# Batch 0 in three blocks of two query tiles, and the hash constant as an exp bias

## The chip, the cores and the metric

The kernel runs on one core of a Trainium2 chip. The time is device microseconds (us) of one execution. TensorE is PE in the profile (PEld its weight loads), VectorE DVE, ScalarE ACT, GpSimd POOL, SyncE SP; SPq is SP's issuing of transfers.

## The reference

Four batches of attention with 8 heads, 768 tokens and 64 dimensions. A query sees only the keys whose six hash bits equal its own. The result is the input of a gated feed-forward layer.

```python
q_bits = (einsum('bhsd,dk->bhsk', q, proj) > 0);  k_bits = likewise
mask   = q_bucket[:, :, :, None] == k_bucket[:, :, None, :]
attn   = softmax(where(mask, q @ k.T / 8, -1e9))
x      = (attn @ v) as [3072 tokens, 512]
out    = x + sigmoid(x @ w_res) * ((gelu(x @ w_gate) * (x @ w_val)) @ w_out)   # d_ff = 1536
```

## The kernel before

Each head has an augmented operand: 64 rows of q or k, 6 rows of hash bits as +-0.5, and a seventh row with a constant. One matmul gives the scaled score plus a bonus for equal bits, and an exp with a large scale makes every unequal pair vanish. Two heads (a pair) are prepared together: 4 pairs in a batch, 16 in all.

The kernel doesn't run its operations as written. `op` records each with a cost and the keys that it reads and writes; at the end a small list scheduler in the kernel plans them with these costs and gives out one order for each engine. On the chip each engine goes through its order and waits on semaphores. So a change of a cost, a key or a latency can change the order of everything.

```python
RINGS = dict(sc=2, av=1, mm=3, qs=3, ks=3, vs=3, trT=4, e=8, bits=4, ...)
LAT = 0.22
...
# the sign column that also makes the constant hash row; the tiles are 4 or 8 bytes wide
for nm, lay in (("shift0", ...), ("shift1", ...)):
    ind = const.tile([P, 2], FP32, name="ind" + nm)
    ...
    sh = const.tile([P, 1], FP32, name=nm)
...
def load_blocks(n):                       # q and k of batches 1 to 3: pieces of 32 floats
    for nm, src in (("q", q), ("k", k)):
        s = stage_of(nm, n, [P, S // Q, Q])
        for hh in range(2):
            for c in range(D // Q):
                load(nm, "SP", g, s, ..., src[b, 2*j+hh, :, c*Q:(c+1)*Q].rearrange("(m p) d -> p m d", p=Q), 0.65, 0.6)
...
def prep_blocks(n):                       # DVE transposes, PE hashes, DVE makes bits, SP moves them
    for side, nm in enumerate("qk"):
        op("DVE", 0.9, nc.vector.transpose(trT()[:, side, :], s()...))
    ...
    for i in range(4):
        op("SP", 0.75, nc.sync.dma_start(a[D:KAUG, :, i*CH:(i+1)*CH], bits()[32*i:32*i+NR]),
           r=[(bits, 0), (bits, 1)],
           w=[("aug", n % NAUG, hh, i // 2, i % 2, "b") for hh in range(2)], size=0.15)
...
# scores of two key tiles against half of the queries (384), then exp
op("ACT", 0.715, nc.scalar.activation(e(), sp()[:, :, 0:CH], AF.Exp, scale=EXPS), r=[sp], w=[e], table="exp")
...
# every batch has two blocks of three query tiles; beside the attention of one block PE does
# the feed-forward of the block before it, which starts with the gates
def end_block(u):
    transpose_x(u)
    for m in range(KF):
        gate(u, m)
    ff = feed_forward(u)
```

The softmax here doesn't subtract the row's maximum and nothing guards it: scores larger than these inputs give would overflow.

## Time and profile before

| | before |
|---|---|
| time | 358.78 us median of 3 (358.62 to 359.25) |
| profiled span | 358.0 us |
| PE, ACT, DVE busy | 343.7, 239.3, 194.4 us |
| first gate matmul | 39.31 us |
| starts of the gates of the next blocks | 82.58, 127.81, 168.58, 211.15, 251.92, 290.87, 328.14 us |

The starts of the gates cut the span into stages of one block each, 40.77 us in the later batches where PE does not wait (the last three are shorter); reading PE's busy time and the length of each stage tells where PE worked and where it idled. Two more views matter for what follows: the stages between the first gates and the gates of batch 1, and the queue of transfers that SP issues. In the stage lines the columns are the stretch, its length, then busy time (and instructions) of PE, weight load, DVE, ACT and POOL, the granted clock, the DMA share and GB/s.

```profile
39.31:82.58 43.27, 42.98 (x415) 25.26 (x413) 29.82 (x48) 30.50 (x45) 3.32 (x4) 1.00 1.04 155
82.58:127.81 45.23, 42.32 (x403) 24.45 (x399) 30.90 (x49) 31.81 (x45) 4.46 (x4) 1.00 1.04 153
```

The queue lines give packets, megabytes, and the time that the packets took as a share of 16 engines' span:

```profile
q1 hardware_dynamic: 101762, 25.54, 38.3%
```

PE idles 3.20 of these 88.50 us, and 2.42 of that is the one stall on xT. The DMA share is 1.04 in both stages.

### The profile page before, as it was taken

Reading aid. Unit: us, or ns where it says so; the run is one execution under the profiler, and the core shown is the slowest. Engines: PE = TensorE matmul, PEld = TensorE weight load, DVE = VectorE, ACT = ScalarE, POOL = GpSimd, SP = SyncE. Lnnn points to the kernel's source line nnn. Section 1 sums busy time; section 2 is a strip of 40 time slices with the busy share of each in tenths; the row PEclk is TensorE's granted clock in tenths of the full one; section 3 lists DMA queues with packets and bytes.
Section 4 is the critical chain, followed back from the end, with each engine's and each line's share of the span. In section 5 each row is a group of like instructions: output and inputs, shape, how many; then the busy total and the mean of one; then the engine's idle time right before and its main releaser. Section 6 shows DMA issues by size and latency. Waiting matters only on the chain.

```text
span 358.0 us, 7849 instructions
## 1 busy us (share of the span) xinstructions
PE 343.7 (96%) x3183; PEld 205.7 (57%) x3183; DVE 194.4 (54%) x356; ACT 239.3 (67%) x344; POOL 24.2 (7%) x35
## 2 busy tenths in 40 slices
PE   7879999999999979999899999999999999999995
PEld 3546665556565546655465566655666566655653
DVE  5897137997794565858063453734153333524353
ACT  2579887558767568676676678685887778776410
POOL 0543001100100100011000000000000000000000
PEclk9999999999999999999999999999999999999999
DMA  7969999779999969920000010000000010001002
GB/s 239 333 124 198 202 169 157 122 126 167 197 117 120 182 111 190 149 64 34 31 1 7 31 66 0 3 33 32 35 0 3 32 59 2 0 31 51 10 2 88
DMA packets 105381, 31.47 MB, mean 88 GB/s; under 512 B 95274, under 2 KB 101378, under 8 KB 105346
## 3 DMA queue, kind: packets, MB, share of 16 engines
q1 hardware_dynamic: 101762, 25.54, 38.3%
q0 software_dynamic: 3280, 5.24, 8.3%
q8 instruction: 25, 0.41, 0.5%
q10 hardware_dynamic: 304, 0.20, 0.2%
q14 instruction: 10, 0.08, 0.1%
HBM read 29.36 MB, written 6.29 MB: 100 GB/s over the span
## 4 chain that ended last, share of the span: by engine, by line
PE 83%; DVE 5%; DMA 4%; ACT 4%; SPq 2%; issue 1%; DVEq 0%; ACTq 0%
PE mm L604 17%; PE mm L619 17%; PE mm L644 16%; PE sc L534 15%; PE av L558 8%; PE mm L631 5%; DMA ks<-in_k_dram 3%; ACT e L538 3%; PE mm L495 2%; SPq L247 2%; PE mm L587 1%; DMA qs<-in_q_dram 1%; DVE aug L397 1%; DVE aug L419 1%; DVE bits L409 1%
## 5 line engine op out<-in xcount | busy, mean ns | idle before, releaser
L538 ACT ACTIVATE e<-sc 128x768 bf16<-128x768 f32 x192 | 150.0, 810 | 57.7 <-PE sc L534 57.6
L534 PE MATMUL sc<-aug 71*128 71x384 bf16 x384 | 91.6, 326 | 1.0 <-ACT e L538 0.7
L622 DVE TENSOR_TENSOR gh<-mm,gh 128x384 bf16<-128x384 f32 x96 | 53.0, 555 | 71.2 <-PE mm L619 58.8
L619 PE MATMUL mm<-xT,wv 128*128 128x384 bf16 x384 | 72.0, 326 | 0.0
L644 PE MATMUL mm<-wo,gh 128*128 128x512 bf16 (+1 forms) x300 | 71.9, 371 | 0.0
L558 PEld LDWEIGHTS <-e 128*128 128x128 bf16 x1152 | 56.2, 97 | 24.6 <-issue 3.0
L604 PE MATMUL mm<-xT,wg 128*128 128x384 bf16 x384 | 65.4, 326 | 3.9 <-DVE xT L593 2.4
L558 PE MATMUL av<-vaug,e 128*128 128x65 bf16 x1152 | 61.7, 193 | 2.1 <-DVE xtok L572 2.1
L607 ACT ACTIVATE gh<-mm 128x384 bf16<-128x384 f32 x96 | 45.7, 491 | 15.8 <-PE mm L604 15.5
L534 PEld LDWEIGHTS <-aug 71*128 71x128 bf16 x384 | 34.8, 98 | 31.5 <-issue 6.8
L604 PEld LDWEIGHTS <-wg 128*128 128x128 bf16 x384 | 36.7, 98 | 27.7 <-DVE xT L593 2.5
L619 PEld LDWEIGHTS <-wv 128*128 128x128 bf16 x384 | 34.7, 98 | 23.5 <-issue 3.7
L644 PEld LDWEIGHTS <-gh 128*128 128x128 bf16 x300 | 26.6, 98 | 22.1
L652 DVE SCALAR_TENSOR_TENSOR y<-th,mm 128x512 f32<-128x512 bf16 (+1 forms) x25 | 16.6, 662 | 38.3 <-PE mm L644 29.5
L634 ACT ACTIVATE th<-mm 128x512 bf16<-128x512 f32 x24 | 14.3, 597 | 17.5 <-PE mm L631 17.5
L631 PE MATMUL mm<-wr,xT 128*128 128x512 bf16 x96 | 24.7, 379 | 0.0
L361 POOL CAST vaug<-vs 128x768 bf16<-128x768 f32 x16 | 15.0, 935 | 138.9 <-DMA vs<-in_v_dram 81.5
L510 DVE TENSOR_SCALAR aug<-trT 64x1536 bf16<-64x1536 f32 x24 | 22.8, 951 | 2.4 <-PE sc L534 2.0
L502 DVE TENSOR_SCALAR bits<-mm,shift 128x384 bf16<-128x384 f32 x24 | 13.7, 613 | 13.7 <-PE mm L495 13.4
L572 DVE TENSOR_TENSOR xtok<-av,rec 128x384 bf16<-128x384 f32 x32 | 17.8, 557 | 1.1
L487 DVE STREAM_TRANSPOSE trT<-ks 128x768 f32<-128x768 f32 x12 | 11.5, 957 | 11.8 <-DMA ks<-in_k_dram 11.8
L654 DVE SCALAR_TENSOR_TENSOR o<-y,xtok 128x512 f32<-128x512 f32 (+1 forms) x25 | 16.8, 670 | 0.8
(52 smaller groups left out, 159.0 us busy)
## 6 DMA issues: line engine op xcount, KB each, us to landing
vs<-in_v_dram SPq DMA_DIRECT2D x16, 384.0 KB
out_dram<-o SPq DMA_DIRECT2D x23, 256.0 KB
qs<-in_q_dram SPq DMA_DIRECT2D x48, 96.0 KB
ks<-in_k_dram SPq DMA_DIRECT2D x48, 96.0 KB
wg<-in_moe_w_gate_dram POOLq DMA_DIRECT2D x4, 384.0 KB, 7.9
wv<-in_moe_w_val_dram POOLq DMA_DIRECT2D x4, 384.0 KB, 8.7
wo<-in_moe_w_out_dram POOLq DMA_DIRECT2D x4, 384.0 KB, 16.4
qs<-in_q_dram SPq DMA_DIRECT2D x3, 384.0 KB
```

Of the source, the lines that this page charges most:

```text
L510: lambda hh=hh: nc.vector.tensor_scalar_mul(a[0:D, hh, :], trT()[hh * D:(hh + 1) * D].rearrange("d s n -> d (s n)"), QKS),
L534: nc.tensor.matmul(sp()[:, x, 0:CH], a[:, S + jt * P:S + (jt + 1) * P], a[:, c * CH:(c + 1) * CH], start=True, stop=True)
L538: op("ACT", 0.715, lambda: nc.scalar.activation(e(), sp()[:, :, 0:CH], AF.Exp, scale=EXPS), r=[sp], w=[e], table="exp")
L558: nc.tensor.matmul(av()[:, o:o + D + 1], e()[:, x, t * P:(t + 1) * P], va[:, 2 * j + hh, TS[b][jt], :], start=(first and x == 0 and t == 0 ...
L572: op("DVE", 0.48, lambda: nc.vector.tensor_mul(xt()[:, :, j * P:(j + 1) * P].rearrange("p t (h d) -> p h t d", h=2), view()[:, :, :, 0:D], ...
L604: nc.tensor.matmul(ps()[:, 0:CH], wg[:, kk, m * P:(m + 1) * P], x()[:, kk, :], start=(kk == 0), stop=(kk == KM - 1))
L607: op("ACT", 0.385, lambda: nc.scalar.activation(g()[:, m, :], ps()[:, 0:CH], AF.Gelu), r=[ps], w=[(g, m)], table="gelu")
L619: nc.tensor.matmul(ps()[:, 0:CH], wv[:, kk, m * P:(m + 1) * P], x()[:, kk, :], start=(kk == 0), stop=(kk == KM - 1))
L622: op("DVE", 0.46, lambda m=m, ps=ps: nc.vector.tensor_mul(g()[:, m, :], ps()[:, 0:CH], g()[:, m, :]), r=[ps], w=[(g, m)])
L631: nc.tensor.matmul(rps(), x()[:, kk, t * P:(t + 1) * P], wr[:, kk, :], start=(kk == 0), stop=(kk == KM - 1))
L644: nc.tensor.matmul(ps()[:, 0:W], g()[:, kk, t * P:(t + 1) * P], wo[:, kk, cols], start=(kk == 0), stop=(kk == KF - 1))
L654: op("DVE", 0.6 / parts, lambda y=y, o=o, t=t, cols=cols, W=W: nc.vector.scalar_tensor_tensor(o()[:, 0:W], y()[:, 0:W], 0.5, xt()[:, t, co ...
```

## The change

The intent is to let the feed-forward start earlier. Batch 0 is cut into three blocks of two query tiles, so that the first block's attention ends sooner; only the queries of the first block must be ready for it, the others are prepared later; the constant hash row gives way to a bias in exp. In the plan, short transfers land 3.5 us after their issue, and the latency between engines goes from 0.22 to 0.26.

```diff
-    NR = NBITS + 1
-    KAUG = D + NR
+    blocks = [(0, c, 2) for c in range(T // 2)] + [(b, c, TC) for b in range(1, B) for c in range(2)]
+    KAUG = D + NBITS
-    RINGS = dict(sc=2, av=1, mm=3, qs=3, ks=3, vs=3, ...
+    RINGS = dict(sc=2, av=1, mm=3, qs=4, ks=3, vs=3, ...
-    LAT = 0.22
+    LAT = 0.26
...
-                    wire = max(wire, o.end + 0.9) + o.size
-                    o.land = wire + 0.9
+                    if o.size > 0.2:
+                        wire = max(wire, o.end + 0.9) + o.size
+                        o.land = wire + 0.9
+                    else:
+                        o.land = o.end + 3.5
...
-    shifts = [] ...                       # the eight instructions and four small tiles of the sign column
+    ebias = const.tile([P, 1], FP32, name="ebias")
+    nc.vector.memset(ebias, -EXPS * NBITS / 4)
...
+    OLD = ["p0", "p1", "late", "h0", "h1", "late0", "late1"]
...                                        # prep_tokens: keys and first queries, then the late queries
-               w=[("aug", n % NAUG, hh, i // 2, i % 2, "b") for hh in range(2)], size=0.15)
+               w=keys_of(n, range(2), OLD + [("q%d", "k%d")[i // 2] % (i % 2)], "b"), size=0.15)
...
-        ... AF.Exp, scale=EXPS)
+        ... AF.Exp, bias=ebias, scale=EXPS)
...
-        loads.setdefault(max(LB, begin[n] - 14), []).append(n)
+        loads.setdefault(max(LB, begin[n] - (24 if n < 2 * NPAIR else 14)), []).append(n)
```

## The prediction

> **What bounds the kernel now.** I read the page's busy line and slices first, then a table of stretches, then the timeline of the first 45 us, then the list of PE waits after 35 us.
>
> ```profile
> PE 343.7 (96%) x3183; PEld 205.7 (57%) x3183; DVE 194.4 (54%) x356; ACT 239.3 (67%) x344; POOL 24.2 (7%) x35
> DMA  7969999779999969920000010000000010001002
> 12.00:20.00 8.00, 7.16 (x107) 4.89 (x107) 7.61 (x17) 4.67 (x8) 2.69 (x4) 1.00 1.09 293
> 20.00:30.00 10.00, 7.83 (x110) 5.34 (x108) 9.59 (x23) 7.16 (x11) 6.39 (x10) 1.00 0.70 126
> ...
> 40.00:80.00 40.00, 39.71 (x377) 23.01 (x376) 27.19 (x45) 28.58 (x42) 3.24 (x4) 1.00 1.05 152
> 120.00:160.00 40.00, 37.58 (x339) 22.52 (x337) 25.86 (x42) 27.74 (x40) 4.03 (x4) 1.00 0.87 141
> 200.00:240.00 40.00, 40.00 (x378) 23.89 (x377) 19.04 (x34) 28.65 (x42) 0.00 (x0) 1.00 0.07 23
> ```
>
> The columns of the stretches are length, then busy time of PE, weight load, DVE, ACT and POOL, the clock, the DMA share, GB/s. Two regimes show. From 40 us PE has no gap worth the name (40.00 of 40 from 200 to 240): PE is the bound, DVE and ACT have room. Before 40 us PE is not the bound although it looks busy, because 72 + 11 of its matmuls there are keep-warm ones that compute nothing; DVE is (9.59 of 10).
>
> ```profile
> 27.37 10.46 ACT L538 ACTIVATE e<-sc 128x768 bf16<-128x768 f32 x14 [2.39 <-PE sc L534]
> 28.11 1.49 DVE L419 COPY aug<-bits 7x384 bf16<-7x384 bf16 x4
> 39.31 0.81 PE L604 MATMUL mm<-xT,wg 128*128 128x384 bf16 x4
> PE mm L604 <- DVE xT L593: 2.4, 1, 2.4
> PE mm L604 <- ACT gh L607: 1.5, 1, 1.5
> L538 ACT ACTIVATE e<-sc 128x768 bf16<-128x768 f32 x192 | 150.0, 810 | 57.7 <-PE sc L534 57.6
> ```
>
> So the prologue has two legs: DVE prepares the four head pairs until 29.6 us, then ACT works off 14 exps back to back (10.46/14 = 0.747 us each) until 37.8, and the first gate matmul, the first feed-forward work that can fill PE, starts at 39.31. After that PE idles 2.4 us once at 125 us (DVE stood behind a late k transfer), 1.5 us once at 170 us, under 1 us elsewhere, and 3.7 us in the tail. Time = start of the gates + PE work left + these stalls.
>
> **What the Trainium skill says.** (1) "TensorE: Matmul & The Clock Gate", "Wait — 56ns, not 53.3ns?": a warm matmul takes N/2.4 ns plus about 2.5 ns. The chain shows 36 gate matmuls of 384 columns in 5.85 us, 162.5 ns each = 160 + 2.5: agrees, so 256 columns should take 109.2 ns. (2) "ScalarE: Activation LUTs", "What ACT_TABLE_LOAD costs": a table load takes about 1283 ns; the trace has 1283 ns (x8 and x7). (3) The same section: 0.833 ns per element plus 186 ns with an immediate bias, and each [128,1] pointer operand adds about 93 ns. The trace has 810 ns at 768 columns and 491 at 384: slope 0.831, fixed part 172, so the exps now run with an immediate bias. The change hands exp a [128,1] tile. No run here shows that cost yet. (4) "VectorE: DVE Perf Modes", "Mode 2×_2P": single-source work from SBUF can go two elements a cycle, from PSUM not. The trace agrees: casts from SBUF gain 0.62 ns per column (599 ns at 768, 360 at 384), evictions from PSUM 1.05 (685 at 512, 550 at 384).
>
> **The change part by part.**
>
> *Removed at the start:* eight small DVE instructions for the sign column, about 1 us between 1.3 and 2.3 us. DVE then waits for the first transpose until 4.86 anyway: worth 0. One hash row less (71 to 70 partitions) changes no instruction's length: 0.
>
> *Preparation on DVE.* For one pair the first part is now two casts of 64x1024, two bit tests of 256 and four moves of 512. From the rates above: 2 x 0.76 + 2 x 0.48 + 4 x 0.36 = 3.9 us; before it was 4 casts, 2 bit tests of 0.61 and 4 moves, about 4.8. Pair 0 (evictions, six half-size casts and so on) I sum to 6.1. To the end of the last pair's first part: 6.1 + 3 x 3.9 + 0.6 for one normalisation = 18.4 us. The same sum for the kernel before gives 23.1 and took 24.7 (4.9 to 29.6), so I expect about 20 and an end near 25. But the built order shows that DVE then prepares the late queries of pairs 0, 1 and 2 before it can evict the second x transpose: 3 x (2 casts 0.88 + 2 bit tests 0.66) + two evictions 1.4 + four normalisations 2.4 + two xT copies 0.8 = 9.2. So DVE is at about 34 when xT is complete; in the kernel before it was there at 40.1 (39.51 + 0.56). **Gates about 6 us earlier, at 33.3.** ACT doesn't forbid it: 24 exps of 512 columns at 0.535 us (0.747 less 256 x 0.83 ns), or 0.63 with the pointer bias, are 13 to 15 us in place of 18.
>
> *PE work that moves behind the gates.* The built order has, ahead of the first gate, 52 scores of 384 and 144 av matmuls before, 56 of 256 and 96 after. Scores: 52 x 162.5 = 8.45 us against 56 x 109.2 = 6.1; totals are 62.4 and 62.5, so 2.4 us more is left. Av (0.18 us per six in the timeline, 30 ns each): 48 more = 1.4. Four x transposes 0.2. Pair 3's late transposes and hash 0.75. The extra fixed 2.5 ns on 48 gate and 48 value matmuls 0.25. **Sum +5.1 us of PE work after the gates.** Net of these two terms: about -1 us. That is the centre of my argument: a shorter first block is no gain in itself, because its attention would have been useful filler that now has to be done later.
>
> *ACT in the region of batch 0.* Three small blocks in place of two: 24 more exps, one more pair of table loads (2.6 us), 12 more gelus, and 93 ns on all 216 exps (20 us if the page holds). In a small block PE has: gates 5.2 + values 5.2 + residual 1.7 + output 5.2 + scores 5.2 + av 2.9 + transposes 0.4 = 26 us and some preparation; ACT has 24 x 0.69 + 12 x 0.38 + 2 x 0.6 + 2.6 + 0.5 = 25.4. So ACT goes from 28.6 of 40 to nearly level with PE for three blocks. PE issues in order and the score ring has two buffers, so I expect 2 to 3 us of new PE waits there, plus up to 1 us at the additional boundary (the built order puts 18 keep-warm matmuls behind the first 12 gates). In the full blocks ACT rises by 24 x 0.093 = 2.2 to about 31 of 40: hidden.
>
> *Transfers.* DMA is full (share about 1.05) from 35 to 140 us in both. Loads of batch 1 are issued 24 steps ahead in place of 14 and get two small blocks, some 54 us in place of 42. The stall at 125 us should shrink or go: -2. Against it, DVE now has batch 1's first transpose right after the first block's 12 products; if that load, gated by wr, is late, DVE blocks in order: +1.
>
> *Sum:* 358.8 - 6.0 + 5.1 + 2.5 + 0.5 - 2.0 + 1.0 = 359.9 taken as it stands. The order was visibly re-tuned (a longer latency in the plan, measured-looking starts), which should keep some of the two stall terms from happening; I take 3 us off for that, a choice and not a sum. **356.8 us.**
>
> **The rivals.**
> A. *Gates still earlier.* If ACT takes more of the late evictions, or the chain runs tighter than my 20 us, gates start at 30 to 31 and the rest holds: 353 to 354. For it: pair 3 is ready at 25. Against it: 9.2 us of DVE work stands ahead of the second xT copy in the order.
> B. *ACT becomes the bound.* If 93 ns fall on each exp and ACT stays on the path in three small blocks and at every boundary: 361 to 364. For it: the 25.4 to 26 above. Against it: 57.7 us of ACT idle before exps, all waiting for PE.
> C. *Transfers hit earlier.* Weights are issued sooner (three wg at once), so pairs 2 and 3 land later and DVE waits in the prologue; gates at 36, time about 359 to 361. For it: the share of 1.09 at 12 to 20 us. Against it: only 0.70 at 20 to 30, while POOL waited for a v tile.
>
> **Range and chances.** Terms that can each move by about 2 us (gate start, ACT waits, transfers) give 352.5 to 361. Faster by over 2% means under 351.6: rival A and the full stall gain together, 0.08. Slower by over 2% means over 366: B and C together and more, 0.05. Within 2%: 0.87.
>
> **What would show it.** In the changed profile: the first gate matmul at 32 to 35 us (over 37: C; under 31: A); exps of 512 columns at about 690 ns and of 768 at about 900 (600 and 810 would refute the pointer cost); ACT busy about 265 to 270 us; no 2.4 us PE wait on xT near 125 us; new PE waits behind ACT between 35 and 120 us of 2 to 3 us in total; full blocks with 39.9 of 40 as now. My prediction is wrong if the prologue's gain isn't given back, that is if the gates start 6 us earlier and the end moves as much.

## The result, and the profile after

The changed kernel took 362.59 us (median of 4 runs, 361.55 to 364.05), the kernel before 359.01 on the same chip (358.62 to 359.77). The ratio is 1.010, 95% interval 1.006 to 1.0139: the same within 2%, but slower, and outside my range. Ratios and their intervals are from the runs of the same rounds; they are not quite the ratio of the medians that are quoted. The profiled spans are 358.0 and 360.9 us.

```profile
PE 344.4 (95%) x3357; PEld 220.9 (61%) x3382; DVE 195.9 (54%) x375; ACT 264.0 (73%) x383; POOL 23.7 (7%) x35
DMA  7999979998579884101000010001000010001002
33.47:62.16 28.69, 28.24 (x327) 22.45 (x327) 16.89 (x36) 23.66 (x42) 1.66 (x2) 1.00 0.95 162
62.16:96.68 34.52, 31.30 (x351) 21.69 (x351) 29.25 (x51) 24.19 (x41) 4.07 (x4) 1.00 0.86 164
96.68:130.08 33.40, 32.29 (x362) 22.62 (x362) 21.85 (x40) 29.14 (x42) 1.66 (x2) 1.00 0.87 162
172.81:213.71 40.90, 40.74 (x384) 24.39 (x384) 16.03 (x33) 31.48 (x43) 0.00 (x0) 1.00 0.06 22
```

The 2.9 us between the spans can be booked from these lines and those of before:

| part | before | after | difference |
|---|---|---|---|
| start to first gate | 39.31 | 33.47 | -5.84 |
| PE busy, first gate to the gates of batch 1's first block | 42.98 + 42.32 = 85.30 | 28.24 + 31.30 + 32.29 = 91.83 | +6.53 |
| PE idle in the same stretch (88.50 and 96.61 us long) | 3.20 | 4.78 | +1.58 |
| from there to the end | 230.19 | 230.82 | +0.63 |

The gates came 5.84 us earlier, and 6.53 us of PE work came to lie behind them. That alone is a small loss. In the changed kernel's trace 25 matmul records are missing (3357 matmuls, 3382 weight loads), so its PE work is shown a little too small and its idle time too large: of the 4.78 us, waits of over 0.25 us make up 4.19, of the 3.20 before 3.07. The last row is the exp: a full block of the quiet batches is now 40.90 us long, 40.77 before. The exps by form show why, 900 ns where there were 810:

```profile
L589 ACT ACTIVATE e<-sc,ebias 128x768 bf16<-128x768 f32 x144 | 125.9, 900 | 34.2 <-PE sc L587 32.0
L589 ACT ACTIVATE e<-sc,ebias 128x512 bf16<-128x512 f32 x72 | 46.4, 687 | 10.4 <-PE sc L587 9.6
```

The idle time after 40 us, from PE's timeline (start, length, what, and in brackets the idle time before it and what ended it):

```profile
64.96 4.09 PE L665 MATMUL mm<-xT,wg 128*128 128x256 bf16 x36 [0.64 <-ACT gh L668]
90.01 0.50 PE L587 MATMUL sc<-aug 70*128 70x384 bf16 x2 [0.78 <-DMA aug<-bits]
94.18 0.34 PE L587 MATMUL sc<-aug 70*128 70x384 bf16 x1 [1.53 <-DMA aug<-bits]
99.69 0.49 PE L665 MATMUL mm<-xT,wg 128*128 128x256 bf16 x3 [0.51 <-ACT gh L668]
```

The 2.42 us on xT are gone, and 0.78 + 1.53 = 2.31 us of waiting for hash bits have come. SP's queue tells where those bits were. The bits of batch 1's first pair were ready on DVE at 72.05 us (71.03 + 1.02), and their four moves went out like this:

```profile
77.19 0.80 SPq L543 DMA_DIRECT2D aug<-bits  x1
78.03 3.16 SPq L256 DMA_DIRECT2D qs<-in_q_dram  x4
...
82.39 0.76 SPq L543 DMA_DIRECT2D aug<-bits  x1
...
87.56 0.76 SPq L543 DMA_DIRECT2D aug<-bits  x1
...
92.13 0.76 SPq L543 DMA_DIRECT2D aug<-bits  x1
```

The lines left out are loads and moves of later pairs; which move belongs to which pair follows from the order that the kernel's own scheduler gives out. The third and fourth move carry the bits of the two halves of k, and PE's two waits end at 90.01 and 94.18 us, 2.45 and 2.05 us after these moves were issued.

In the kernel before the four moves of a pair stood in a row:

```profile
66.12 3.52 SPq L505 DMA_DIRECT2D aug<-bits  x4
```

### The profile page after: what moved, and what is told of

The parts are those of the page before. It is cut to its first block, busy times and chain, and to the rows that moved or that the text cites. A ratio compares the mean times of both kernels' runs of the same rounds, so it can differ in the third digit from the quotient of the medians.

```text
span 360.9 us, 8331 instructions
## 1 busy us (share of the span) xinstructions
PE 344.4 (95%) x3357; PEld 220.9 (61%) x3382; DVE 195.9 (54%) x375; ACT 264.0 (73%) x383; POOL 23.7 (7%) x35
## 3 DMA queue, kind: packets, MB, share of 16 engines
q1 hardware_dynamic: 101794, 25.47, 31.1%
## 4 chain that ended last, share of the span: by engine, by line
PE 83%; DVE 6%; ACT 5%; DMA 2%; issue 2%; SPq 1%; ACTq 0%; DVEq 0%
PE mm L706 17%; PE mm L681 17%; PE mm L665 17%; PE sc L587 15%; PE av L614 8%; PE mm L693 5%; ACT e L589 3%; PE mm L533 2%; DVE aug L419 2%; DMA ks<-in_k_dram 2%; DVE aug L431 2%; PE mm L647 1%; ACT L668 1%; DVE bits L425 1%; SPq L256 1%
## 5 line engine op out<-in xcount | busy, mean ns | idle before, releaser
L589 ACT ACTIVATE e<-sc,ebias 128x768 bf16<-128x768 f32 (+1 forms) x216 | 172.2, 829 | 44.6 <-PE sc L587 41.6
L684 DVE TENSOR_TENSOR gh<-mm,gh 128x384 bf16<-128x384 f32 (+1 forms) x108 | 55.1, 511 | 80.3 <-PE mm L681 76.5
L587 PE MATMUL sc<-aug 70*128 70x384 bf16 (+1 forms) x432 | 95.2, 308 | 3.3 <-DMA aug<-bits 2.3
L681 PE MATMUL mm<-xT,wv 128*128 128x384 bf16 (+1 forms) x432 | 73.0, 308 | 0.0
L665 PE MATMUL mm<-xT,wg 128*128 128x384 bf16 (+1 forms) x432 | 65.9, 308 | 2.5 <-ACT gh L668 2.5
L587 PEld LDWEIGHTS <-aug 70*128 70x128 bf16 x432 | 38.3, 98 | 32.5 <-issue 6.6
L668 ACT ACTIVATE gh<-mm 128x384 bf16<-128x384 f32 (+1 forms) x108 | 47.3, 455 | 12.4 <-PE mm L665 10.1
L540 DVE TENSOR_SCALAR bits<-mm 128x384 bf16<-128x384 f32 x24 | 12.2, 548 | 15.0 <-PE mm L533 15.0
L630 DVE TENSOR_TENSOR xtok<-av,rec 128x384 bf16<-128x384 f32 (+1 forms) x36 | 18.5, 513 | 1.2
L653 ACT COPY xT<-mm 128x768 bf16<-128x768 bf16 (+1 forms) x8 | 6.2, 772 | 9.4 <-PE mm L647 9.4
```

The lines of the kernel that those rows point to most:

```text
L587: nc.tensor.matmul(dst, a[:, kc[x]:kc[x] + P], qs, start=True, stop=True)
L589: op("ACT", 0.105 + 0.0008 * 2 * W, lambda: nc.scalar.activation(e()[:, :, 0:W] if b else e().rearrange("p x n -> p (x n)")[:, 0:2 * W], s ...
L630: op("DVE", 0.08 + 0.14 * tiles, lambda: nc.vector.tensor_mul(xt()[:, 0:tiles, j * P:(j + 1) * P].rearrange("p t (h d) -> p h t d", h=2), ...
L665: nc.tensor.matmul(ps()[:, 0:W], wg[:, kk, m * P:(m + 1) * P], x()[:, kk, 0:W], start=(kk == 0), stop=(kk == KM - 1))
L668: op("ACT", 0.08 + 0.0008 * W, lambda: nc.scalar.activation(g()[:, m, 0:W], ps()[:, 0:W], AF.Gelu), r=[ps], w=[(g, m)], table="gelu")
L681: nc.tensor.matmul(ps()[:, 0:CW], wv[:, kk, m * P:(m + 1) * P], x()[:, kk, 0:CW], start=(kk == 0), stop=(kk == KM - 1))
```

## The experiments

A caution for the profiles below: in those of e2, e8, e9, e13 and e18 the granted clock of the stretch before the first gate was 0.95 or 0.96 in place of 1.00, and that gate came 1 to 3 us late (at 36.51 in e9, against 33.47 in the changed kernel). In e5 it was 0.95 too, with the gate in time. So the stages behind the first gate are compared, not the spans.

### First theories: the pointer bias, and work put behind the gates

**e1_imm** gives exp its constant as an immediate and drops the tile:

```diff
-    ebias = const.tile([P, 1], FP32, name="ebias")
-    nc.vector.memset(ebias, -EXPS * NBITS / 4)
-  ... AF.Exp, bias=ebias, scale=EXPS)
+  ... AF.Exp, bias=-EXPS * NBITS / 4, scale=EXPS)
```

> The changed kernel with the exp bias as a number in the instruction in place of the [128,1] tile; the order of instructions on every engine is the same. Theory A (the pointer bias is part of the loss, though ACT is not the bound on average): exps fall to about 594 and 807 ns, ACT busy falls by about 20 us, the first gate matmul starts 1 to 1.5 us earlier (the last 11 exps before it run back to back at 0.676 us), the PE waits behind ACT at the small blocks' gates shrink, and the full blocks lose the 0.13 us by which each is longer (40.90 against 40.77); the time falls by 2.5 to 3.5 us, to about 359.5. Theory B (ACT's longer exps lie beside PE work): the time falls by less than 0.7 us.

Measured: 366.7 us, ratio 1.0192 (1.0149 to 1.0235), where the changed kernel has 1.010: about 3.3 us slower than with the pointer. The exps did go back to 810 and 597 ns and the full blocks to 40.77. The loss sits in one stage, with a wait of 4.54 us for bits and a lower clock:

```profile
61.94:101.35 39.41, 33.08 (x354) 22.21 (x351) 28.83 (x51) 22.16 (x41) 3.95 (x4) 0.96 0.99 151
94.49 0.82 PE L585 MATMUL sc<-aug 70*128 70x384 bf16 x2 [4.54 <-DMA aug<-bits]
```

Both theories missed. The cause was found only with the last runs; I first put it down to SP's queue.

**e2_before_ptr** puts a zero bias tile into the kernel before, and nothing else:

```diff
+    ebias = const.tile([P, 1], FP32, name="ebias")
+    nc.vector.memset(ebias, 0.0)
-  ... AF.Exp, scale=EXPS)
+  ... AF.Exp, bias=ebias, scale=EXPS)
```

> The kernel before with a [128,1] tile of zeros as the exp bias and nothing else. Theory A: exps at about 902 ns; the 14 exps back to back ahead of the first gate take 1.3 us more, each boundary about 0.1 more: 361 to 361.5 against 359. Theory B: under 0.7 us slower.

Measured: 359.88 us, ratio 1.0001 (0.9952 to 1.005). Full blocks grew from 40.77 to 40.89, as in the change, but the 2.42 us stall vanished: the stage that had been 45.23 us was 42.31. I took it that slower exps gave the transfers time. The last runs speak against that reading: e17 below has fast exps and short transfers too.

**e3_early** starts the preparation of batch 1 twelve steps earlier, so that the bits are early:

```diff
-        begin[n] = at - LB + 2 + 6 * j if b == 1 else ...
+        begin[n] = at - LB - 10 + 6 * j if b == 1 else ...
```

> The changed kernel with batch 1's preparation placed 12 steps earlier in the record. Theory C (the 2.3 us of PE waits for hash bits at 90 to 94 us come from batch 1's preparation being crowded into the last small block): both waits go, the time falls by 2 to 2.5 us, to about 360.3. Rival D (DMA is the limit there: 0.86 to 0.95 share, so the wait turns up elsewhere): the PE idle time from the first gate to batch 1's first gate stays at 4.8 us and the time within 0.7 us.

Measured: 365.63 us, ratio 1.0177 (1.0128 to 1.0227). The waits for bits went, and the time went up: PE now waited 0.60 us for a transpose of a load at 60.70, and after more short gaps the clock fell:

```profile
67.00:68.00 1.00, 0.80 (x11) 0.60 (x9) 0.70 (x1) 1.00 (x3) 0.00 (x0) 1.00 1.01 169
68.00:69.00 1.00, 0.74 (x9) 0.39 (x7) 0.67 (x3) 0.98 (x3) 0.00 (x0) 0.78 1.07 243
69.00:70.00 1.00, 1.00 (x8) 0.80 (x8) 1.00 (x2) 0.62 (x1) 0.00 (x0) 0.50 1.17 352
```

At a granted clock of 0.50 matmuls take twice as long (in e6 two scores of 384 columns took 0.64 us from 111.22, and 0.33 at full clock), so a short wait costs more than itself. The Trainium skill says, in "TensorE: Matmul & The Clock Gate", "What's actually happening", that throttled is the default state and that the clock is half after an idle window of about 3.4 us. The trace of e6 below agrees: PE idle from 104 to 108 us, a clock of 0.50 from 110 to 112. Here PE was busy for most of the time ahead of the fall (3.15 of the 4 us from 65 to 69), which that idle window doesn't tell; what set it off stays open.

**e4_warm33** tells the plan that the gates start at 33 us in place of 35, which leaves out 18 keep-warm matmuls that had come to lie behind the first gates:

```diff
-    arrange(35.0, keep_warm)
+    arrange(33.0, keep_warm)
```

> The changed kernel without the 18 keep-warm matmuls that stand behind the first 12 gate matmuls (44 in all instead of 62). If they delay the next gates: 36 gate matmuls start 0.5 to 0.9 us earlier and the time falls by as much. If PE waits for the first gelu there anyway: same within 0.3 us.

Measured: 362.36 us, ratio 1.0076 (1.0032 to 1.012): unchanged. The stage was 0.7 us shorter (27.98 for 28.69), so the keep-warm matmuls do cost that. But the two waits for bits behind it grew from 0.78 and 1.53 to 1.50 and 1.71: the gain was waited away.

### Second theory: a false chain between the moves of the bits

The change's four moves of a pair all write the same OLD keys. The plan therefore has each wait for the landing of the one before, which the change sets to 3.5 us; the moves write different columns, so the data don't need that. SP follows the planned order, so the moves get spread between loads. **e5_unchain** lets one operation without cost write the OLD keys, and each move its own key only:

```diff
+        op("SP", 0.0, lambda: None, w=keys_of(n, range(2), OLD, "b") + [("aug", n % NAUG, "old")])
-               r=[(bits, 0), (bits, 1)], w=keys_of(n, range(2), OLD + [...], "b"), size=0.15)
+               r=[(bits, 0), (bits, 1), ("aug", n % NAUG, "old")],
+               w=keys_of(n, range(2), [("q%d", "k%d")[i // 2] % (i % 2)], "b"), size=0.15)
```

> The changed kernel, but the four hash-bit moves of one head pair no longer all write the same old keys, so the plan no longer thinks each must wait for the landing of the one before; on SP they stand four in a row again. Theory F (the false chain delays batch 1's bits and is what turned a small gain into a loss): the two waits of scores for the bits near 90 and 94 us (0.78 and 1.53) are gone, gate starts at 33.5 and 62 as before, the third small block's stretch is near 32.3 instead of 33.4 to 34.5, time about 360 (2 to 2.5 us under the changed kernel). Rival D (the transfers are full until 140 us, so the bits are late whatever the order): a wait of 1.5 us or more for aug, trT or xT turns up again between 60 and 110 us, time within 0.7 us of the changed kernel.

Measured: 364.34 us, ratio 1.0108 (1.0074 to 1.0143). The theory fell. Its mechanism was there: both waits for bits vanished and the stage shrank from 34.52 to 31.87 us. But the next stage grew from 33.40 to 37.31:

```profile
94.14:131.45 37.31, 34.50 (x362) 23.32 (x362) 21.43 (x40) 29.36 (x42) 1.66 (x2) 0.95 0.88 164
95.39 3.19 SPq L544 DMA_DIRECT2D aug<-bits  x4
98.63 1.00 SPq L256 DMA_DIRECT2D ks<-in_k_dram  x2
97.00:100.00 3.00, 2.75 (x23) 1.96 (x23) 0.98 (x1) 0.85 (x3) 0.00 (x0) 0.63 0.11 23
103.32 0.98 DVE L525 STREAM_TRANSPOSE trT<-ks 128x768 f32<-128x768 f32 x1 [5.34 <-DMA ks<-in_k_dram]
```

While SP issues four moves in a row (3.19 us, 9 KB each), the load of k stands behind them and the DMA engines run dry: share 0.11, 23 GB/s. DVE takes its work in order and stands 5.34 us before the transpose of that k. The start of the next gates also lost 1.7 us later (42.58 for 40.90 us in the stage from 174 us), which belongs to the new order of the plan.

**e6_unchain_imm** adds the immediate bias to e5, **e7_unchain_imm_warm** the start of 33.0 as well.

> The same without the chain and with the exp bias as an immediate. Theory F: exps back at about 810 and 600 ns, full blocks at 40.77 instead of 40.90, no wait for the bits, so 6 x 0.13 + up to 0.7 in the small blocks: about 1 to 1.5 us under the run without the chain, 358 to 359. With the chain the same edit cost 4 us more (366.7), which theory F puts down to the wait of 4.5 us for the bits and the fall of the clock after it. Rival D: a wait for transfers of over 2 us in the third small block comes again and the time is 362 or more.

> The same again, and the plan's start for the gates set to 33.0, which leaves out the 18 keep-warm matmuls behind the first gates. Theory F: 0.7 us under the run before it, 357.5 to 358.3, so a little faster than the kernel before. Rival D: no better than that run, because the saved time is spent in waits for transfers.

Measured: 369.09 us (ratio 1.0244, 1.0195 to 1.0292) and 368.06 us (1.0214, 1.0181 to 1.0246), the slowest of all. In e6 DVE stood behind k loads for 3.65 and 4.85 us, PE behind DVE, and the clock fell:

```profile
104.00:106.00 2.00, 0.00 (x0) 0.00 (x0) 0.00 (x0) 1.68 (x3) 0.00 (x0) 1.00 0.91 217
106.00:108.00 2.00, 0.00 (x0) 0.00 (x0) 0.95 (x2) 0.00 (x0) 0.00 (x0) 1.00 1.05 225
110.00:112.00 2.00, 2.00 (x12) 1.29 (x11) 1.10 (x3) 0.00 (x0) 0.23 (x1) 0.50 1.59 143
```

**e8_before_chain** is the converse: the kernel before with the false chain put in.

```diff
-    w=[("aug", n % NAUG, hh, i // 2, i % 2, "b") for hh in range(2)], size=0.15)
+    w=[("chain", n)] + [("aug", n % NAUG, hh, i // 2, i % 2, "b") for hh in range(2)], size=0.16)
+    # and in the plan: a transfer of size 0.16 lands 3.5 us after its issue
```

> The kernel before with the false chain put in: its four bit moves of one pair all write one more shared key, and the plan lands such a move 3.5 us after its issue; nothing else. Theory F: SP issues batch 1's moves singly between loads, new waits of scores for aug of 1 to 3 us between 80 and 130 us, time 1 to 3 us over the kernel before. Rival D: the bits were bound by the transfers anyway; time within 0.7 us of the kernel before.

Measured: 360.86 us, ratio 1.0009 (0.9975 to 1.0043): no loss. A chained order is different, not worse: a wait for bits of 0.98 us and two waits at the gates of 84 us (0.96 and 1.13) had come, and the 2.42 us stall on xT was gone.

### Third theory: the transfers themselves, or SP's queue

**e9_cheap_after** and **e10_cheap_before**: Their outputs are wrong, which doesn't matter for the times. The q and k loads of batches 1 to 3 fetch as many bytes in as many instructions, but in pieces of 3072 bytes in place of 128. The orders of the engines stay.

```diff
-  src[b, 2*j+hh, :, c*Q:(c+1)*Q].rearrange("(m p) d -> p m d", p=Q), 0.65, 0.6)
+  src[b, 2*j+hh].rearrange("(p x m) (y d) -> x p (m y) d", x=D//Q, p=Q, y=D//Q)[c], 0.65, 0.6)
```

> Wrong result on purpose: the changed kernel, whose q and k loads of batches 1 to 3 fetch the same number of bytes in the same number of instructions, but in pieces of 3072 bytes instead of 128; the order of the instructions on every engine is the same. Theory G1 (the transfers of these small pieces are the limit until 140 us, so that each stall taken away early comes back later): DMA share between 36 and 130 us falls from 0.9 to under 0.5, the waits of scores for the bits (0.78 and 1.53) and waits on trT go, time 2 to 3 us under the changed kernel. Theory G2 (the limit is SP, which issues loads and bit moves one after another): issue times on SP stay, the waits stay, time within 0.7 us.

> Wrong result on purpose: the same edit on the kernel before, same order of instructions. Theory G1: the stall of 2.42 us on xT at 127 us goes, gates at 39.3 as before, time 2 to 2.5 us under the kernel before, so 356.5; the distance to the changed kernel with the same edit stays about 2 to 3 us, as more PE work behind the gates (6.5 us) than the gates are earlier (5.8). Theory G2: the stall stays, time within 0.7 us.

Measured: 358.23 us (ratio 0.9932, 0.9854 to 1.001) and 355.33 us (0.9865, 0.9797 to 0.9932); the kernel before took 360.24 in these rounds. The waits for bits and the stall on xT went, each kernel gained more than the 2 to 3 us expected (4.9 us between the medians for the kernel before, 4.4 for the changed one, on different chips), and most of the distance between the two stayed: 2.9 us by the medians, 2.4 by the ratios, though with overlapping intervals. Part of the unexpected gain of e10 is the gate wait of 1.47 us at 171 us, which had gone as well (that stage took 40.90 us in place of 42.57). So transfers in short pieces cost both kernels several us, and they are not the main thing that sets them apart.

**e11_pool_after** and **e12_pool_before** have the bit moves of batches 1 to 3 issued by POOL in place of SP:

```diff
-            op("SP", 0.75, lambda i=i: nc.sync.dma_start(a[D:KAUG, :, ...
+            op("POOL", 0.75, lambda i=i: nc.gpsimd.dma_start(a[D:KAUG, :, ...
```

> The changed kernel with the hash-bit moves of batches 1 to 3 issued by POOL (idle 93% of the time) instead of SP; PE and ACT orders are the same. Theory G2: SP gains 3.1 us per head pair, the bits no longer stand behind loads and the loads no longer behind bits: both waits for bits and any wait on trT go, time 2 to 3 us under the changed kernel. Theory G1: the bits waits go, but DVE waits for a q or k load somewhere between 95 and 130 us and the time is within 1 us of the changed kernel.

> The same on the kernel before. Theory G2: the stall of 2.42 us at 127 us goes and the time is about 356.5, faster than both kernels. Theory G1: the stall stays or moves, time within 0.7 us of the kernel before.

Measured: 360.83 us (ratio 1.0034, 0.9949 to 1.0118) and 358.52 us (0.9945, 0.987 to 1.0021). In the changed kernel the waits for bits went without a new one in their place:

```profile
61.72:93.58 31.86, 30.96 (x351) 21.75 (x351) 28.35 (x51) 24.06 (x41) 10.41 (x18) 1.00 1.01 191
```

31.86 us against 34.52: SP's queue did hold the bits and the loads up. The intervals are too wide to give the gain in time a size.

### What is left when transfers don't bind, and a wrong control

**e13_cheap_imm_warm** is e9 with the immediate bias and the start of 33.0. **e14_pool_imm** is e11 with the immediate bias, **e15_pool_imm_warm** that with the start of 33.0. **e16_pool_before** is e12 in more rounds.

> Wrong result on purpose: the changed kernel with the cheap transfers, the immediate bias and no keep-warm matmuls behind the gates. If the rest of the difference is the terms of my sum, it loses 0.13 in each of five full blocks, up to 0.5 at the boundaries of the small blocks and 0.7 of keep-warm: about 356.3 to 356.8, still about 1 us over the kernel before with cheap transfers (355.33), which is PE work moved (5.1) plus one more boundary (0.5) less the gates' gain (5.5). If the pointer bias is the main cause, it is at or under 355.3.

> The changed kernel with the bit moves on POOL and the immediate bias. Theory G2 (the SP queue is what turned the immediate bias into a loss): full blocks 40.77 in place of 40.90 and less waiting for exps in the small ones, 0.7 to 1.2 us under the run with POOL alone (360.83), so 359.6 to 360.1. Theory G1 (the transfers themselves pin the point near 100 us): a wait for transfers of 1 us or more comes in and the time is the same or more.

> The same without the 18 keep-warm matmuls behind the gates. G2: another 0.7 us less, 358.9 to 359.4. G1: no gain, the time goes into a wait for transfers.

> The kernel before with the bit moves on POOL, again and with more rounds beside the others, to settle whether it beats both kernels: about 1.7 us under the kernel before (ratio 0.995), and under e15.

Measured: e13 355.78 us, ratio 0.9864 (0.9827 to 0.9901), beside 0.9865 (0.9797 to 0.9932) for the kernel before with cheap transfers. No difference is shown; the two intervals together leave room for an estimated 2.8 us either way. The profiles say much the same: from the first gate to the end e13 takes 320.53 us and e10 313.87, 6.66 more, and the changed kernel's gates start 5.84 us earlier. So with transfers out of the way, an immediate bias and no keep-warm matmuls behind the gates, the three small blocks gain nothing that these runs can show. The pointer bias and the keep-warm matmuls together are the step from 0.9932 to 0.9864, again with overlapping intervals; from the first gate to the end the profiles of e9 and e13 differ by 2.06 us (322.59 and 320.53), of which 0.7 is the keep-warm matmuls of e4.

e14 364.12 us (1.0101, 1.0071 to 1.0132) and e15 364.11 (1.0104): the immediate bias again came with a loss, 0.7% or 2.4 us against e11 (whose interval reaches 1.0118), with POOL moving the bits; the stage before batch 1's gates took 38.32 us in place of 33.39. So SP's queue wasn't the reason either. e16 359.74 us, 0.9965 (0.9927 to 1.0003): the gain of e12 shrank to a third of a per cent, and isn't shown.

### Fourth theory: where the tiles lie

Every run with an immediate bias had dropped the 4-byte tile too. In the memory map of the built programs, that tile takes 32 bytes, and all later tiles move. With it the q and k staging tiles start at multiples of 64 bytes; in the kernel before, and in e1, e6, e7, e14 and e15, they start 32 bytes off (so too in e8, e10, e12, e13 and e16). **e17_imm_aligned** keeps the tile, which nothing reads any more, and makes the bias immediate:

```diff
     ebias = const.tile([P, 1], FP32, name="ebias")
     nc.vector.memset(ebias, -EXPS * NBITS / 4)
-  ... AF.Exp, bias=ebias, scale=EXPS)
+  ... AF.Exp, bias=-EXPS * NBITS / 4, scale=EXPS)
```

> The changed kernel with the immediate bias, but with the 4-byte bias tile kept though nothing reads it: orders of all engines as in the changed kernel, the staging tiles at multiples of 64 bytes as there. Theory P (placement): the load queue's share is 31% as in the changed kernel, not 35.2% as with the immediate bias alone; no fall of the clock near 100 us; exps 810 and 600 ns, full blocks 40.77; time 0.7 to 1.5 us under the changed kernel, so 361 to 362, 5 us under e1. Rival: the pointer bias itself shaped the transfers by slowing ACT; then the share is 35%, and the time 366 as in e1.

Measured: 361.09 us, ratio 1.0065 (1.002 to 1.011); e1, the same kernel 32 bytes off, had 1.0192. The load queue of the changed kernel, of e1 and of e17, in this order:

```profile
q1 hardware_dynamic: 101794, 25.47, 31.1%
```
```profile
q1 hardware_dynamic: 101794, 25.47, 35.2%
```
```profile
q1 hardware_dynamic: 101794, 25.47, 31.4%
```

Same packets, same bytes: 31.1% of 360.9 us is 112 us of all 16 engines, 35.2% of 364.6 is 128, 31.4% of 358.5 is 113. And the stage in which e1 lost:

```profile
61.45:95.26 33.81, 31.13 (x351) 21.65 (x351) 29.78 (x51) 22.14 (x41) 3.32 (x4) 1.00 0.86 166
```

33.81 us against 39.41, without a fall of the clock. So the placement, not the bias, made e1 slow. All runs with loads in short pieces fall into the same two groups: with the tile the queue's share is 30.8 to 31.8% (eight programs, the changed kernel among them), without it 34.6 to 38.3% (nine, the kernel before among them). The trace's packet records tell which transfers grew: a packet of 128 bytes (q and k) took 12.8 ns on average in the changed kernel, 15.2 in e1 and 12.7 in e17, and 16.3 in the kernel before. So the change had, without meaning to, also put its staging tiles in the better place. e2 fits (31.8%, 12.9 ns): its tile had moved the staging tiles, and that is the likely reason why its stall vanished. The kernel before with the unused tile alone, which would show it, wasn't run.

The Trainium skill, "DMA: Bandwidth & Descriptors", "How a descriptor splits into AXI transactions", says that a transaction starts at a 256-byte boundary, so that a descriptor which doesn't costs more beats. It speaks of bytes fetched; what is off here is the destination. The direction agrees. But the median packet of 128 bytes took 13 ns in both e1 and e17, and only the slowest tenth grew, from 13 ns to 24 and more; added beats on every packet would have moved the median. So the mechanism stays open.

**e18_pool_before_aligned** puts the unused tile into e16.

> The kernel before with its bit moves on POOL and an unused 4-byte tile that puts the staging tiles at multiples of 64 bytes. Theory P: the load queue's share falls from 37.8% to about 31%, the second stretch between gate starts from 44.06 to about 42.1 and the first from 44.17 to 43.3, time 2 to 3 us under the kernel before, about 357, with the run with cheap transfers (355.33) as a floor. Rival: no change against e16 (share 37.8%, 359.7).

Measured: 359.72 us, ratio 0.9991 (0.9962 to 1.002). The queue did what was expected, in e16 and then e18:

```profile
q1 hardware_dynamic: 100754, 25.02, 37.2%
```
```profile
q1 hardware_dynamic: 100754, 25.02, 31.3%
```

The time didn't follow: the two stages stayed 44.17 and 44.07 us. With POOL moving the bits no DVE transpose waited for a load between 30 and 150 us in e16 already, so faster loads were worth nothing. What makes these stages long is in their order: one gate wait of 1.47 us moved there from 171 us, another 0.45 us behind exp.

No run is shown to beat the kernel before with a right result; e12 and e16, the same kernel twice, come nearest, and both intervals reach 1. The changed kernel with POOL moves, immediate bias and kept tile wasn't run. An estimate from e11's 1.0034 and the step from 1.010 to 1.0065 puts it at 1.000.

## Why the prediction was wrong

**The gates.** Predicted 33.3, measured 33.47. The number was right, the path to it only in part. I had DVE set the start, with 9.2 us of late queries and copies ahead of the complete xT, and ACT with time to spare. DVE was through with the late queries at 30.59 us and then waited for PE and the exps, 1.34 us before the last normalisation and 0.67 before the last copy, while ACT went from 26.76 to 34.20 without a pause:

```profile
26.76 7.44 ACT L589 ACTIVATE e<-sc,ebias 128x512 bf16<-128x512 f32 x11 [0.71 <-PE sc L587]
32.36 0.18 DVE L629 RECIPROCAL rec<-av 128x4 f32<-128x4 f32 x1 [1.34 <-PE av L614]
```

So the exps held the end of the prologue, and part of the hit is luck. Their lengths were right: about 900 and 690 ns predicted, 900 and 687 measured, ACT 264.0 us (265 to 270 predicted). The Trainium skill, "ScalarE: Activation LUTs", "What ACT_TABLE_LOAD costs", says about 93 ns for a pointer operand; 810 to 900 ns is 90.

**PE work behind the gates.** +5.1 predicted, +6.53 measured. The keep-warm matmuls behind the gates are 0.7 of the gap (e4); I saw them in the built order and counted them inside "up to 1 us at the additional boundary". The other 0.7 stays open. It is not in the counts behind the gates: 56 scores of 384 columns and 88 of 256 against 100 of 384 are +2.5 us at the prediction's rates, 342 av matmuls against 300 are +1.3. The centre of the argument, that a shorter first block is no gain in itself, fits e13 against e10, 0.9864 and 0.9865, within their intervals.

**ACT.** +2.5 in the small blocks and +0.5 at the boundary predicted; the waits behind ACT in the timeline are 0.29 + 0.64 + 0.51 + 0.44 = 1.9. I wrote that in the full blocks the pointer is hidden. It isn't quite: 0.13 us a block, 0.63 to the end. From first gate to end, e17 is 1.8 us shorter than the changed kernel (325.63 against 327.43), and e9 and e13 leave 1.4 for it; so much the pointer cost in the profiles. The ratios of the changed kernel and e17, 1.010 and 1.0065, have overlapping intervals.

**Transfers.** -2.0 for the stall at 125 us was right as a line; the reason that I gave isn't shown. I credited loads issued 24 steps ahead; e2, with the loads where they had been, lost the stall as well, most likely by 32 bytes of placement. No run separates the two in the changed kernel. And I had no term for what replaced it, 2.31 us of waiting for bits. Their order came with the key list and the 3.5 us landing, both in plain sight in the diff. e5 shows that undoing it alone is no gain: with the bits in time, the loads came late on the same SP queue.

**The step that failed** is the last: "The order was visibly re-tuned (a longer latency in the plan, measured-looking starts), which should keep some of the two stall terms from happening; I take 3 us off for that, a choice and not a sum." The sum as it stood was 359.9, 1.1 over the kernel before; the spans gave 2.9 over. The 3 us off turned a small loss into a gain. The stall terms of the sum were 2.5 + 0.5 for ACT and 1.0 for a late load, 4.0 us, of which I kept 1.0. What the runs showed in its place: 1.88 us of waits behind ACT and 2.31 for the bits came, 4.19 in all, so the changed plan kept none of them away. It also put 18 keep-warm matmuls behind the gates. Of its reordered variants e3 was slower (1.0177) and e5 no faster (1.0108); e6 and e7 were slower too, but had their staging tiles moved as well.

**The rivals.** B (361 to 364, ACT) has the time, but only part of the cause: the pointer is 1.4 to 1.8 of it. C (transfers hit earlier) was there in small, a wait of PE of 1.80 us for a k tile that ended at 18.23, with the gates on time. The range failed because it was centred on the choice.

## What to carry to other kernels

Work out what an earlier start leaves for later before counting it as a gain: if the bound engine must do the same work, filler removed ahead of the start comes back behind it. Don't take an optimistic guess off a sum; a plan that was re-tuned can have new stalls as well as fewer. And when an experiment removes a tile, see where all the others then lie: a control that moves the staging buffers is no control.

## What the Trainium skill lacked or had wrong

- "DMA: Bandwidth & Descriptors": no figure for where in SBUF short pieces land. Here the load queue took 34.6 to 38.3% of the engines' span with 128-byte pieces into tiles 32 bytes off a multiple of 64, at a multiple of 64 bytes 30.8 to 31.8%, for the same 25 MB; in e1 and e17 that is 128 against 113 us. Its split of descriptors is told for fetched bytes only.
- The same page, on issuing engines: it names issue time, but gives no figure for what small transfers cost the loads behind them. Four moves of 9 KB held SP 3.19 us in e5, and the DMA share fell to 0.11.
- "TensorE: Matmul & The Clock Gate": no figure for how little idle time lowers the clock. The idle window of "What's actually happening" fits e6 (0.50 from 110 to 112 us, after 4.43 us of idle PE); in e3 the clock went to 0.50 at 69 us though PE had been busy 0.80 and 0.74 of the two us ahead. A later section of the page, on a second failure mode, has the clock fall from frequent short idles too, without such a figure.
